# A residual quantizer with four residual buffers and a written-out order, with x stored by group and transposed two groups at a time

## The chip, the cores and the metric

The kernel runs on one core of a Trainium2 chip. The metric is the device time of one execution in microseconds; a lower time is better. TensorE is PE, VectorE is DVE, ScalarE is ACT, GpSimd is POOL and SyncE is SP in the rows of the profile.

## The reference

A depthwise convolution of three taps over time, a SiLU, four stages of residual vector quantization with eight words each, and a second depthwise convolution. The input is 2 x 16000 tokens of 512 channels in bfloat16.

```python
z = silu(conv3(x, dw_enc))                 # B=2, T=16000, D=512
res, q = z, 0
for s in range(4):                         # Nq = 4 codebooks
    cb = codebooks[s]                      # 8 words of 512
    d2 = (res*res).sum(-1) - 2*res @ cb.T + (cb*cb).sum(-1)
    sel = cb[d2.argmin(-1)]
    q, res = q + sel, res - sel
y = conv3(q, dw_dec)
```

## The kernel before, in words

The 32,000 tokens are split over 128 rows of 250 tokens. A *group* is one token of each row (128 tokens), and the 250 groups are cut into 17 *chunks* (`SIZES`, L24): 4 groups, 12 groups, fourteen times 16, and 10. A chunk's data stands with channels on the 128 partitions, in four blocks `i` of 128 channels, and the tokens along the free dimension.

Each chunk passes through these steps.

- *Load* (`load`, L419). Each group is brought by a DMA that transposes (L428), on SP's queue, into `XT`, a buffer of 34 groups by block. The first two chunks come as rows and are transposed by PE (`load_rows`, L392). `again` (L444) copies the two groups that two chunks share.
- *Front* (`front`, L464), for each block `i`: three products with the taps on VectorE (L486), written to a `Z` tile and `T` tiles. The first `SPLIT[i]` of the two additions are accumulating DMAs on POOL's queue (L497); the others are VectorE's. The second addition on VectorE (L500) writes the *residual* buffer `RES`, and so is the step that takes one of the three residual buffers. Then ScalarE makes exp (L508) into an `E` tile, VectorE adds one (L512), ScalarE takes the reciprocal (L184; exp and reciprocal need different tables, loaded by ACT_TABLE_LOAD), and VectorE multiplies (L518).
- *Stage* `s` (`stage`, L562), four times: PE computes for every 64 tokens the products with the eight words and with the tokens themselves (`score`, L584 for a mask and L590). ScalarE takes the norms (L601), VectorE casts the products (`dots`, L620), PE sums both (L604, L611), VectorE casts the sums (`VT`, L616). POOL makes the key with four operations: L658, L645, L647, L662. VectorE finds the least and the one-hot (L666, L672). PE and ScalarE turn the one-hots into pairs of words (L715, L720, L727, L733), PE selects the words (L749), and VectorE adds them to the residual: four *updates* (L755), one for each block. The fourth stage has no updates; after its scores, the residual buffer is free.
- *Finish* (`finish`, L805): PE decodes from the one-hots (L773), ScalarE copies to `YSB` (L779), and SP stores (L783).

Every operation is a task of `Plan` (L63) with an engine, a duration, the tasks that it needs, and a due time, which is the chunk's `START` plus the step's `OFF` (L38 to L60). `Plan.run` plays the tasks through while the program is built: an engine that is free takes the ready task with the earliest due time for which the buffers (`slots`) suffice. Each engine's instructions then stand in that order, and every engine works strictly in its order. Where PE has nothing to do in this play, `warm` (L382) puts in matmuls of 512 columns whose result is not used (L387), until PE is busy for the share `WARM` of 3.4 us.

The buffers are counted at L219: `plan = Plan({"Z": ZB, "T": TB, "E": EB, "Y": YB, "ps": 4, "RES": 3, "OH": 3})`, with four each of Z, T, E. A residual buffer holds for every 64 tokens 16 code columns, 64 tokens, and 16 code columns (96 columns).

Of the kernel before, what the change touches and what calls it, by code (L numbers as in the profile page):

```python
# [10 lines left out]
BF16 = mybir.dt.bfloat16  # L11
# [9 lines left out]
LC = 16  # L21
ROOM = 2 * GC + 2

SIZES = [4, 12] + [16] * 14 + [10]  # L24
# [5 lines left out]
WARM = 0.4  # L30
SPLIT = (1, 1, 1, 2)
RELU = (0, 1, 2, 3)

ZB, TB, EB, YB = 4, 4, 4, 2
# [3 lines left out]
START = [-49.78, -21.21, -11.1, 40.29, 77.41, 126.87, 171, 213.64, 259.89, 295.9, 339.35, 382.88, 414.63, 449.59, 490.48, 512.46, 542.77]  # L38
OFF = {
    "words": -209.08, "codes": -112.52, "col0": -187, "sums": -87.73, "mask": -228.88, "norms": -202.91, "col1": 18.74,  # L40
# [19 lines left out]
}  # L60


class Plan:  # L63

# [12 lines left out]
    def run(self):  # L77
# [3 lines left out]
        for n, t in enumerate(tasks):  # L81
            for d in t[3]:
                after[d].append(n)
# [789 lines left out]
```

## Time and profile before

| | us |
|---|---|
| median of 3 runs | 815.28 |
| lowest and highest run | 812.22 and 817.3 |
| the profiled execution | 809.59 |
| its span, first to last instruction | 807.8 |

The profile is that of the execution of 809.59 us; 1.8 us of it lie around the span. A row of the groups gives the line, the engine, the operation, what is written and read, the count, then the busy time and the mean of one, then the idle time of the engine just before. A row of the timeline begins with the start and the length. A window's row gives its bounds and length, the busy time and count of each engine, the granted clock of PE as a share of the full clock, the busy share of the DMA engines, and GB/s.

### The profile page before, as it was taken

Reading aid. Unit: us, or ns where it says so; the run is one execution under the profiler, and the core shown is the slowest. Engines: PE = TensorE matmul, PEld = TensorE weight load, DVE = VectorE, ACT = ScalarE, POOL = GpSimd, SP = SyncE. Lnnn points to the kernel's source line nnn. Section 1 sums busy time; section 2 is a strip of 40 time slices with the busy share of each in tenths; the row PEclk is TensorE's granted clock in tenths of the full one; section 3 lists DMA queues with packets and bytes.
Section 4 is the critical chain, followed back from the end, with each engine's and each line's share of the span. In section 5 each row is a group of like instructions: output and inputs, shape, how many; then the busy total and the mean of one; then the engine's idle time right before and its main releaser. Section 6 shows DMA issues by size and latency. Waiting matters only on the chain.

```text
span 807.8 us, 28980 instructions
## 1 busy us (share of the span) xinstructions
PE 622.8 (77%) x13019; PEld 381.0 (47%) x13092; DVE 628.2 (78%) x1027; ACT 538.6 (67%) x571; POOL 284.9 (35%) x459
## 2 busy tenths in 40 slices
PE   3065787877878878887799877878885759889985
PEld 3023454544444544535356545554553526446543
DVE  5998889896988798878778897887969785855530
ACT  2345748494789477697847976866937596793553
POOL 1244353442534155426243452253414342212200
PEclk9568788999989999989999998998998979989989
DMA  4749677767796777895967778768984542121231
GB/s 150 112 83 153 130 133 134 124 121 164 141 207 147 164 145 175 136 176 117 166 153 121 203 139 184 128 140 153 187 158 68 105 121 93 47 92 44 80 157 79
DMA packets 149542, 107.71 MB, mean 133 GB/s; under 512 B 130217, under 2 KB 131370, under 8 KB 149290
## 3 DMA queue, kind: packets, MB, share of 16 engines
q1 hardware_dynamic: 137796, 66.62, 37.4%
q0 software_dynamic: 11472, 39.10, 27.0%
q8 instruction: 102, 1.67, 0.9%
q14 instruction: 22, 0.18, 0.1%
q10 hardware_dynamic: 150, 0.13, 0.1%
HBM read 3.70 MB, written 32.77 MB: 45 GB/s over the span
## 4 chain that ended last, share of the span: by engine, by line
PE 28%; DVE 19%; ACT 14%; issue 8%; POOL 7%; DMA 3%; ACTq 0%; another core or an unknown queue 0%; DVEq 0%; POOLq 0%
PE PS L590 12%; DVE RES L755 10%; PE PS L749 5%; ACT YSB L779 4%; PE PS L584 4%; ACT E L184 3%; PE PS L773 3%; PE PS L611 2%; ACT E L508 2%; POOL S L645 2%; ACT L L601 2%; POOL D L658 2%; DVE RES L500 2%; DMA out_dram<-YSB 2%; DVE T L486 1%
## 5 line engine op out<-in xcount | busy, mean ns | idle before, releaser
L755 DVE TENSOR_TENSOR RES<-RES,PS 128x2048 bf16<-128x2048 bf16 (+2 forms) x204 | 224.5, 1136 | 26.0 <-PE PS L749 25.6
L590 PE MATMUL PS<-RES 128*64 128x80 bf16 (+1 forms) x8064 | 204.2, 208 | 36.7 <-DVE RES L518 26.7
L590 PEld LDWEIGHTS <-RES 128*64 128x64 bf16 x8064 | 170.1, 118 | 93.9 <-issue 31.7
L601 ACT ACTIVATE L<-PS 128x512 bf16<-128x512 f32 (+2 forms) x132 | 75.8, 577 | 168.5 <-PE PS L590 90.4
L749 PE MATMUL PS<-POH,PAIR 64*128 64x512 bf16 (+2 forms) x1224 | 158.4, 396 | 33.6 <-DVE RES L755 14.6
L779 ACT ACTIVATE YSB<-PS 128x1024 bf16<-128x1024 f32 (+1 forms) x126 | 124.6, 1019 | 15.3 <-PE PS L773 8.9
L184 ACT ACTIVATE E<-E 128x2048 bf16<-128x2048 bf16 (+2 forms) x68 | 120.5, 1786 | 6.6 <-DVE E L512 6.4
L658 POOL TENSOR_TENSOR D<-VT,GPOS 128x128 bf16<-128x128 bf16 (+2 forms) x68 | 45.9, 675 | 204.1 <-DVE VT L616 204.0
L749 PEld LDWEIGHTS <-PAIR 64*128 64x128 bf16 x1224 | 61.9, 102 | 103.5 <-issue 61.4
L497 POOL DMA_DIRECT2D Z<-T x75 | 73.0, 1012 | 102.7 <-issue 28.1
L508 ACT ACTIVATE E<-RES 128x2048 bf16<-128x2048 bf16 (+2 forms) x53 | 92.3, 1755 | 15.1 <-DVE RES L500 12.7
L486 DVE TENSOR_SCALAR T<-XT,WENC 128x2048 bf16<-128x2048 bf16 (+2 forms) x136 | 98.8, 739 | 3.4 <-DMA Z<-T 3.4
L773 PE MATMUL PS<-A,OHT 128*128 128x512 bf16 x224 | 80.9, 398 | 23.6 <-ACT OHT L707 5.9
L584 PE MATMUL PS<-MASK,IDENT 128*128 128x256 bf16 (+2 forms) x264 | 76.1, 288 | 12.1 <-DVE RES L755 6.0
L678 POOL COPY OH<-OH 128x128 bf16<-128x128 bf16 (+2 forms) x68 | 37.8, 562 | 121.8 <-DVE OH L672 121.7
L620 DVE CAST PR<-PS 128x64 bf16<-128x64 f32 (+2 forms) x132 | 28.8, 220 | 65.2 <-PE PS L590 50.5
L518 DVE TENSOR_TENSOR RES<-RES,E 128x2048 bf16<-128x2048 bf16 (+2 forms) x53 | 59.0, 1123 | 8.7 <-ACT E L184 8.7
L645 POOL TENSOR_SCALAR S<-VT,GMIN 128x16 f32<-128x16 bf16 (+2 forms) x68 | 51.4, 755 | 34.6 <-DVE VT L616 34.3
L500 DVE TENSOR_TENSOR RES<-Z,T 128x2048 bf16<-128x2048 bf16 (+2 forms) x53 | 63.4, 1203 | 0.1
L773 PEld LDWEIGHTS <-OHT 128*128 128x128 bf16 x373 | 32.6, 101 | 63.4 <-issue 30.2
L486 DVE TENSOR_SCALAR Z<-XT,WENC 128x2048 bf16<-128x2048 bf16 (+2 forms) x68 | 50.1, 744 | 0.2
L611 PEld LDWEIGHTS <-L 64*64 64x64 bf16 x2016 | 38.2, 111 | 20.9 <-issue 14.3
(103 smaller groups left out, 676.3 us busy)
## 6 DMA issues: line engine op xcount, KB each, us to landing
Z<-T POOLq DMA_DIRECT2D x70, 512.0 KB, 6.0
out_dram<-YSB SPq DMA_DIRECT2D x61, 512.0 KB
XT<-in_x_dram SPq DMA_TRANSPOSE x233
Z<-T POOLq DMA_DIRECT2D x5, 384.0 KB, 5.1
RES<-in_x_dram SPq DMA_DIRECT2D x1, 1536.0 KB
YSB<-in_codebooks_dram SPq DMA_DIRECT2D x12, 64.0 KB
RES<-in_x_dram SPq DMA_DIRECT2D x1, 640.0 KB
out_dram<-YSB SPq DMA_DIRECT2D x1, 384.0 KB
```

What stands on the lines that cost most here:

```text
L184: nc.scalar.add_instruction(mybir.InstActivation(name=nc.get_next_instruction_name(), engine=mybir.EngineType.Activation, ins=args, outs=[ ...
L486: nc.vector.tensor_scalar(out=u[name][:, 0:G, :], in0=XT[:, i, at + k:at + k + G, :], scalar1=WENC[:, i, k:k + 1], scalar2=None, op0=ALU.mult)
L497: nc.gpsimd.dma_start(out=z, in_=t, accum_op=ALU.add)
L500: nc.vector.tensor_tensor(out=u["R"], in0=halves(u["Z"]), in1=halves(u["ZTU"[k]]), op=ALU.add)
L508: nc.scalar.activation(halves(u["E"]), halves(u["Z"]) if adds == 2 else u["R"], ACT.Exp, scale=-1.0)
L584: nc.tensor.matmul(V[:, b, :, own:own + HT], lhsT=IDENT, rhs=MASK[:, 0:m // 2, :], start=True, stop=False, skip_group_check=True)
L590: nc.tensor.matmul(V[h * HT:(h + 1) * HT, b, r, :], lhsT=half[:, LC:LC + HT], rhs=half[:, lo:hi], start=False, stop=(i == KT - 1), skip_gr ...
L601: nc.scalar.activation(u["L", q][:, 0:m, :].rearrange("p (b r) t -> p b r t", b=2), u["V", q][:, :, :, own:own + HT], ACT.Relu)
L749: nc.tensor.matmul(u["SEL", i][:, h, 0:H * HT], lhsT=PAIR[s][rows, part, i * P:(i + 1) * P], rhs=u["POH"][rows, 0:H, :], start=(part == 0) ...
L755: nc.vector.tensor_tensor(out=tokens, in0=tokens, in1=words, op=ALU.add)
L773: nc.tensor.matmul(Y[:, h, :], lhsT=lhs(), rhs=rhs, start=(a == 0), stop=(a == len(terms) - 1))
L779: nc.scalar.activation(u["YSB"][:, k:k + n, :], u[k][:, 0:n, :], ACT.Copy)
```

## The change

The tasks stay the same in kind; what changes is where they run, in which order, and where data lies.

- Order. `START`, `OFF` and the choice by due time go. `ORDER` is a list of all task numbers, and `Plan.run` emits the tasks in it. Tiles are handed out at that time: the one of a kind that is free first.
- Buffers. There are four residual buffers (`RESN`). Their pitch falls from 96 to 80 columns for 64 tokens, since the code columns of even and odd half-groups alternate. The `E` tiles go: exp, plus one and reciprocal work in place in `Z`, of which there are seven.
- x. `XT` has the group outside, `[P, ROOM, KT, P]` for `[P, KT, ROOM, P]`, and a transfer brings two groups (`JOIN = 2`).
- Front. In chunks 2 to 15, one addition of each block is a DMA and one is VectorE's (before, block 3 had two DMAs), and the third product of blocks 2 and 3 runs on POOL (`POOLED`): 28 products. The last chunk has no product on POOL.
- Stage. The casts `dots` are ScalarE's in stages 0 and 2 (`CASTS`), and one of VectorE's or ScalarE's covers ten columns of eight. POOL's addition `S` (L645) goes: the smallest norm lies in a column of `PR` that the matmul of `total` sums. `total` starts with two matmuls of 64 rows instead of one of 128.
- PE's filling matmuls go (`WARM = 0`).
- Setup. The code columns and a part of the pair words are ScalarE's, the clearing of the decoder's tiles is POOL's, and VectorE clears PSUM once.

Line numbers of the changed kernel that are named below: products L548, the DMA add L560, the second add L562, plus one L573, silu L579, exp L570, reciprocal L224, scores L665 and L659, casts L678 and L676, `VT` L705, key L710, L714, L718, updates L817.

VectorE's order where the residual buffers turn over, before. RES_103 is the buffer, L755 the updates, L500 the add that takes the buffer for a new chunk.

```order
L755 TENSOR_TENSOR RES_103<-RES_103,PS 128x32x64 x2
L666 TENSOR_REDUCE M<-T 128x16
L755 TENSOR_TENSOR RES_103<-RES_103,PS 128x32x64
L620 CAST PR_120<-PS 128x8x8
L672 TENSOR_TENSOR OH_10494<-T,M 128x2x8x8
L486 TENSOR_SCALAR T_10496<-XT,WENC 128x2048
L620 CAST PR_120<-PS 128x8x8
L620 CAST PR_121<-PS 128x8x8
L616 CAST VT<-PS 128x144
L620 CAST PR_121<-PS 128x8x8
L500 TENSOR_TENSOR RES_103<-Z,T_10012 128x32x64
```

Between the last update of the old chunk and the first add of the new one stand four casts of scores and one product. VectorE's order at a turn of a buffer after the change; RES_138 is taken again while RES_137, RES_139 and RES_140 hold other chunks (L817 the updates, L562 the add).

```order
L817 TENSOR_TENSOR RES_138<-RES_138,PS_91 128x32x64
L548 TENSOR_SCALAR Z_103<-XT,WENC 128x2048
L722 TENSOR_REDUCE M<-KEY 128x16
L548 TENSOR_SCALAR Z_108<-XT,WENC 128x2048
L725 TENSOR_TENSOR OH_131<-KEY,M 128x2x8x8
L817 TENSOR_TENSOR RES_140<-RES_140,PS_90 128x32x64
L548 TENSOR_SCALAR Z_106<-XT,WENC 128x2048
L678 CAST PR_125<-PS_91 128x10x8
L562 TENSOR_TENSOR RES_138<-Z_104,T_110 128x32x64
```

Three products and an update of another chunk now stand there. Counted over the whole order, 163 of the 204 updates stand ahead of the last chunk's first add, and 172 before the change.

POOL's order in the middle, before: the key's operations (L658, L645, L647, L662), notes of one-hots (L678) and DMA issues (L497).

```order
L678 COPY OH_123<-OH_5579 128x16x8
L497 DMA Z<-T_5122 128x2048
L645 TENSOR_SCALAR S<-VT,GMIN 128x16
L647 TENSOR_TENSOR T<-S,STEP 128x128
L662 TENSOR_TENSOR T<-D_5584,T 128x128
L497 DMA Z<-T_5616 128x2048
L678 COPY OH_124<-OH_5769 128x16x8
L658 TENSOR_TENSOR D_5982<-VT,GPOS 128x128
```

The same after the change: the key is L710, L714, L718, the note L732, the DMA issue L560, and L548 are products.

```order
L560 DMA Z_105<-T_113 128x2048
L732 COPY OH_126<-OH_129 128x16x8
L548 TENSOR_SCALAR T_111<-XT,WENC 128x2048
L548 TENSOR_SCALAR T_110<-XT,WENC 128x2048
L710 TENSOR_TENSOR D_5075<-VT,GPOS 128x128
L714 TENSOR_TENSOR KEY<-VT,STEP 128x128
L710 TENSOR_TENSOR D_5081<-VT,GPOS 128x128
L718 TENSOR_TENSOR KEY<-D_5081,KEY 128x128
```

Two products of 2048 elements stand ahead of the next chunk's key; the S operation is gone.

The diff, cut to its core:

```diff
-SIZES = [4, 12] + [16] * 14 + [10]
+SIZES = (4, 12) + (16,) * 14 + (10,)
-WARM = 0.4
-SPLIT = (1, 1, 1, 2)
-ZB, TB, EB, YB = 4, 4, 4, 2
-START = [-49.78, -21.21, -11.1, ...
-OFF = { "words": -209.08, ...
+WARM = 0.0
+SPLIT = ((0, 0, 0, 0), (0, 0, 0, 0), (1, 1, 1, 1), (1, 1, 1, 1))
+POOLED = ((0, 0, 0, 0), (0, 0, 0, 0), (0, 0, 1, 1), (0, 0, 0, 0))
+JOIN = 2
+CASTS = (True,False,True,False)
+PSB, ZB, TB, YB, LB, POHB, RESN = 4, 7, 4, 2, 2, 2, 4
+ORDER = """
+0 40 349 351 350 38 26 30 36 34 28 32 352 8 353 355 20 357 359 9 354 179 356 358 21 ...
...
 class Plan:
+    def run(self):
+        until, end, spans = {}, {}, []
+        free = {k: [(0.0, t) for t in tiles] for k, tiles in self.free.items()}
+        order = [int(n) for n in ORDER.split()]
+        for n in order:
+            engine, hold, delay, needs, _, emit, take, give, use = self.tasks[n]
+            begin = max([until.get(engine, 0.0)] + [end[d] for d in needs])
+            for k in take:
+                at, self.held[n, k] = free[k].pop(min(range(len(free[k])), key=lambda j: free[k][j][0]))
+                begin = max(begin, at)
...
-    XT = const.tile([P, KT, ROOM, P], BF16, name="XT")
-        t = const.tile([P, KT, 2 * GC, NC + HT], BF16, name=f"RES{n}")
+    XT = const.tile([P, ROOM, KT, P], BF16, name="XT")
+        t = const.tile([P, KT, 2 * GC * WD + LC], BF16, name=f"RES{n}")
...
-            nc.sync.dma_start_transpose(out=XT[:, :, at + n, :], in_=group_rows(g0 + n - 1))
+        def some(n, m):
+            nc.sync.dma_start_transpose(out=XT[:, at + n:at + n + m, :, :].rearrange("p n k t -> p (n k) t"),
+                                        in_=bass.AP(tensor=xf.tensor, offset=xf.offset + (g0 + n - 1) * D, ap=[[S * D, P], [1, m * D]]))
...
-                nc.vector.tensor_scalar(out=u[name][:, 0:G, :], in0=XT[:, i, at + k:at + k + G, :], scalar1=WENC[:, i, k:k + 1],
+                (nc.gpsimd if k == 2 and pooled else nc.vector).tensor_scalar(out=plan.held[u[k], "Z" if k == 0 else "T"][:, 0:G, :], in0=XT[:, at + k:at + k + G, i, :],
...
-                u["E"] = epool.tile([P, GC, P], BF16, name="E")
+            def e():
+                return plan.held[u[2], "T"] if adds == 2 else z()
...
-            nc.gpsimd.tensor_scalar(out=u["S"][:, 0:G], in0=u["TR"][:, 0:G], scalar1=GMIN[:, s:s + 1], scalar2=None, op0=ALU.add)
+            if CASTS[s]:
+                nc.scalar.activation(dst, src, ACT.Copy)
+            else:
+                nc.vector.tensor_copy(dst, src)
```

More of the change, by code (lines that the diff above doesn't have):

```diff
@@ L415, in load_rows @@
-        st["loaded"] = moved + (chunks[0]["loaded"] if st["n"] else [])
-        if st["n"]:
-            codes.append(plan.add("DVE", 1.2, 1.4, moved + codes[0:1], (1, "col2"), lambda: code_columns(RESB[2])))
+            t = took[i] = plan.add("PE", 0.12 * N, 0.12 * N + 0.2, [rows], (n, "rows"), lambda i=i: turn(i), take=("ps",))
+            dve = i % 2 and n == 0
+            hold = (0.08 if dve else 0.12) * N
+            moved.append(plan.add("DVE" if dve else "ACT", hold, hold + 0.1, [t], (n, "rows"), lambda i=i: move(i), give=((t, "ps"),)))
@@ L419, in load @@
+        st["loaded"] = moved + (chunks[0]["loaded"] if n else [])
+        if n:
+            codes[2] = plan.add("ACT", 2.0, 2.2, moved + [words], (1, "col2"), lambda: code_columns(RESB[2]))
+    reads = {p: [] for p in range(ROOM)}
     def load(st):
@@ L552, in block @@
-            return rest
+                    t = plan.add("POOL", 0.9, 0.9, needs, due, lambda: total(k))
+                    return plan.add("DMA", 3.0 * f, 3.0 * f + 2.0, [t], due, None, give=give)
+                first = k == 2 and "RES" not in st
+                if k == 2:
+                    needs = needs + [st["RES"] if not first else chunks[n - 1]["RES"] if 0 < n < RESN else None]
+                t = plan.add("DVE", dve(1.13), dve(1.13) + 0.1, needs, due,
+                             lambda: total(k), take=("RES",) if first else (), give=give)
@@ new lines, in add_up @@
+                if first:
+                    st["RES"] = t
+                return t
+            hold, delay = dve(0.66), dve(0.66) + 0.1
+            for k in range(2):
+                u[k] = plan.add("DVE", hold, delay, st["loaded"], (n, f"{'ztu'[k]}{i}"), lambda k=k: product(k), take=("ZT"[k],))
+            a = add_up(1, [u[0], u[1]])
+            u[2] = plan.add("POOL" if pooled else "DVE", 0.1 + 2.2 * f if pooled else hold, 0.2 + 2.2 * f if pooled else delay, st["loaded"] + [u[1]], (n, f"u{i}"),
+                            lambda: product(2), take=("T",))
@@ L761, in stage @@
+            new.append(plan.add("DVE", 0.07 + 1.06 * f, 0.17 + 1.06 * f, [c] + seen, (n, f"U{s}{i}"), lambda i=i: update(i), give=((c, "ps"),)))
+        plan.add("FREE", 0.0, 0.0, [u["X", i] for i in range(KT)], (n, f"P{s}"), None, give=((t, "POH"),))
         st["new"] = new
-    kept = {}
     def outputs(groups, needs, n, m):
```

662 lines of the change are left out of this document (306 added, 356 removed), and 117 rows, old and new, of tables (OFF, ORDER).

## The prediction, made before the changed kernel had run

> **What bounds the kernel now.** I read the page's busy times first, then the windows, then VectorE's timeline around the residual buffers. No engine is full:
>
> ```profile
> span 807.8 us, 28980 instructions
> PE 622.8 (77%) x13019; PEld 381.0 (47%) x13092; DVE 628.2 (78%) x1027; ACT 538.6 (67%) x571; POOL 284.9 (35%) x459
> ```
>
> So something other than an engine sets the pace. The windows by stage (busy us of PE, PEld, DVE, ACT and POOL, then granted clock and DMA share; cut at the first residual add of chunk 2 and of chunk 16) and two windows of VectorE alone:
>
> ```profile
> 0.00:74.00 74.00, 30.16 (x356) 19.16 (x360) 63.57 (x158) 27.73 (x30) 22.09 (x42) 0.75 0.61 122
> 74.00:695.40 621.40, 497.58 (x10889) 306.45 (x10946) 510.94 (x777) 444.66 (x456) 245.04 (x367) 0.91 0.74 144
> 695.40:807.80 112.40, 95.09 (x1777) 55.37 (x1786) 53.74 (x95) 66.25 (x85) 17.74 (x51) 0.93 0.21 82
> ...
> 20.00:60.00 40.00, 38.77 (x85) 0.59 0.56 97
> 100.00:200.00 100.00, 84.26 (x138) 0.92 0.76 138
> ```
>
> VectorE is 97% busy from 20 to 60 us, while residual buffers are still free, and 82% (510.94 / 621.4) once all three are taken. The timeline says why. Chunk 7 takes the buffer of chunk 4, chunk 8 that of chunk 5, chunk 13 that of chunk 10; the rows show the old chunk's last update (L755), the last scores that read it (L590), and the new chunk's first add (L500):
>
> ```profile
> 326.20 3.47 DVE L755 TENSOR_TENSOR RES<-RES,PS 128x2048 bf16<-128x2048 bf16 x3
> 330.21 1.22 DVE L500 TENSOR_TENSOR RES<-Z,T 128x2048 bf16<-128x2048 bf16 x1
> ...
> 421.73 3.47 DVE L755 TENSOR_TENSOR RES<-RES,PS 128x2048 bf16<-128x2048 bf16 x3
> 426.01 0.77 PE L590 MATMUL PS<-RES 128*64 128x80 bf16 x32
> 426.95 1.22 DVE L500 TENSOR_TENSOR RES<-Z,T 128x2048 bf16<-128x2048 bf16 x1
> ...
> 544.63 2.34 DVE L755 TENSOR_TENSOR RES<-RES,PS 128x2048 bf16<-128x2048 bf16 x2
> 552.24 0.94 PE L590 MATMUL PS<-RES 128*64 128x80 bf16 x32
> 553.37 2.35 DVE L500 TENSOR_TENSOR RES<-Z,T 128x2048 bf16<-128x2048 bf16 x2
> ```
>
> Each buffer is taken again within 0.3 us of the end of its last scores (426.78 to 426.95; 553.18 to 553.37). A chunk comes every (695.4 - 74) / 14 = 44.4 us, so a buffer turns around in 3 x 44.4 = 133 us. VectorE needs only 510.94 / 14 = 36.5 of the 44.4. The buffers bound the middle; the last 112 us belong to PE (95.09 of 112.4, 85%).
>
> **The change part by part.** I cost it as VectorE's work W up to chunk 16's first add, divided by its busy share, and PE's work behind that. Today W = 63.57 + 510.94 = 574.5; 10.4 us of the first stretch are idle (74 - 63.57), and in the rest the share is 574.5 / (695.4 - 10.4) = 84%.
>
> ```profile
> L486 DVE TENSOR_SCALAR T<-XT,WENC 128x2048 bf16<-128x2048 bf16 x112 | 85.7, 777 | 3.4 <-DMA Z<-T 3.4
> L500 DVE TENSOR_TENSOR RES<-Z,T 128x2048 bf16<-128x2048 bf16 x42 | 54.5, 1304 | 0.1
> L620 DVE CAST PR<-PS 128x64 bf16<-128x64 f32 x112 | 24.8, 223 | 53.4 <-PE PS L590 42.8 <-ACT L L601 10.1
> L249 DVE COPY RES<-CBT 128x2048 bf16<-128x2048 bf16 x3 | 2.3, 778 | 0.0
> L250 DVE COPY RES<-CBT 128x2048 bf16<-128x2048 bf16 x3 | 3.1, 1039 | 0.0
> L331 DVE COPY YSB<-PAIR 128x512 uint16<-128x512 uint16 x3 | 1.4, 458 | 0.1
> L342 DVE COPY YSB<-YSB 128x512 uint16<-128x512 uint16 x3 | 1.3, 439 | 0.0
> ```
>
> VectorE loses 28 products to POOL (28 x 0.777 = -21.8), gains 14 second adds that the POOL queue's accumulating DMA did (14 x 1.304 = +18.3), gives 56 of 112 casts to ACT (-12.5), and the setup copies of the last four rows (-8). The new memsets of PSUM fall into its idle start: 0.
>
> POOL's products are not shown before. The nearest rows are a copy of half the size, same type, and a two-input one of 512 f32; and VectorE beside POOL's long operations:
>
> ```profile
> L444 POOL COPY XT<-XT x7: 1027/1037/2072, 54.4 to 551.5; 128x1024 bf16<-128x1024 bf16 x7
> L344 POOL TENSOR_TENSOR PAIR<-YSB 128x512 bf16<-128x512 f32 x3 | 5.0, 1664 | 0.0
> ...
> 42.75 1.57 POOL L344 TENSOR_TENSOR PAIR<-YSB 128x512 bf16<-128x512 f32 x1
> 43.13 1.62 DVE L486 TENSOR_SCALAR Z<-XT,WENC 128x1536 bf16<-128x1536 bf16 x1
> 44.67 0.61 DVE L486 TENSOR_SCALAR T<-XT,WENC 128x1536 bf16<-128x1536 bf16 x1
> ...
> 205.36 2.07 POOL L444 COPY XT<-XT 128x1024 bf16<-128x1024 bf16 x1
> 205.32 1.21 DVE L500 TENSOR_TENSOR RES<-Z,T 128x2048 bf16<-128x2048 bf16 x1
> 206.84 1.67 DVE L500 TENSOR_TENSOR RES<-Z,T 128x2048 bf16<-128x2048 bf16 x1
> ```
>
> Length: 2 x 1.037 = 2.1 us, bounded above by 4 x 1.664 = 6.7; I take 2.1, one input and the same type. Beside POOL's 1.57 us, VectorE's product grew by 1.01 us (64% of it); beside its 2.07 us, an add grew by 0.46 (22%). I take the mean, 43%: 28 x 2.1 x 0.43 = +25, between 0 (POOL runs while VectorE reads PSUM) and the whole, +59. What the offload saves is lost to this. The Trainium skill, page "SBUF — State Buffer", section "Who interferes with whom", calls the port pair that VectorE and GpSimd share an exclusive lock; the 1.62 us row agrees. Taken as the whole length of every product it gives a rival of its own, below.
>
> The fourth buffer moves the front ahead: in the new order VectorE stands at 163 updates of 204 when chunk 16 makes its first add, and at 172 in the old. Nine updates leave W, each 1.2 us with 0.3 of its stage's casts: -13. W = 574.5 - 21.8 + 18.3 - 12.5 - 8 + 25 - 13 = 562.5.
>
> The share is the main choice. Its ends are 84% (as now) and 97% (20 to 60 us, buffers free). With four buffers, a turn of 133 us would allow a chunk every 33 us, less than the 36.5 that VectorE needs, so the buffers stop binding and engines wait for each other instead: PE would be at 475 / 625 = 76%, ACT near 72%. I take 90%, halfway: 562.5 / 0.90 = 625, and with the idle start 635.4 against 695.4.
>
> ```profile
> 74.00:695.40 621.40, 22.61 (x60) 6.50 (x71) 0.91 0.74 144
> 695.40:807.80 112.40, 5.06 (x17) 1.69 (x19) 0.93 0.21 82
> 695.40:807.80 112.40, 34.56 (x32) 0.93 0.21 82
> ```
>
> These are the filling matmuls (L387: 22.61 and 5.06 us of PE) and the updates left at the end (L755: 32). The fillers go; where they stood PE is idle anyway, so I count nothing. The tail has 41 updates for 32. PE's useful 90.0 us there are 2.81 an update: 41 x 2.81 = 115, at the same 85%: 136 us against 112.4. The front's lead is partly given back here.
>
> Covered edits:
>
> ```profile
> L428 SPq DMA_TRANSPOSE XT<-in_x_dram x233: 1190/1269/3372, 23.0 to 604.2; - x117
> 33.69 0.69 DVE L250 COPY RES<-CBT 128x2048 bf16<-128x2048 bf16 x1
> L184 ACT ACT_TABLE_LOAD x24 | 30.8, 1283 | 0.4
> L720 ACT ACTIVATE OHT<-PS 128x128 bf16<-128x128 f32 x42 | 11.5, 274 | 9.5 <-PE PS L715 9.4
> L645 POOL TENSOR_SCALAR S<-VT,GMIN 128x16 f32<-128x16 bf16 x56 | 44.7, 799 | 26.7 <-DVE VT L616 26.4
> ```
>
> - Half as many transposes move the same bytes; SP is the only queue that they pass, and VectorE's products wait for none of them now (their only idle time, 3.4 us, is for Z<-T). If each double one took as long as two, nothing changes; the cover is that x lies a chunk ahead.
> - Products read 16 runs of 128 instead of one of 2048. L250 writes runs of 16 at 0.69 us for 2048, no slower than the products: 0. The upper end, the 1.304 of an add, would be +0.53 a product.
> - ACT gets 66 casts (274 ns: +18) and some 12 us of setup copies; table loads fall from 47 to 33 (14 x 1.283: -18). It has room.
> - POOL loses S (-51 with the small forms) and 15 DMA issues, and gets 59 us of products. Stage steps queued behind two products in a row come up to 4 us late; with four chunks in flight another chunk is ready.
>
> Sum: 635.4 + 136 + 1.8 around the span = 773, against 809.6 for the profiled execution. The median of the runs, 815.28, is 0.7% above that execution, so I predict 778.
>
> **The rivals.** (a) *Slower: POOL's products stop VectorE for long.* For: the 1.62 us row, and that an instruction with a scalar from memory is not in the trace. The gain is gone when W reaches 595, that is at 2.1 us of stopped VectorE for each product. At 4 us and 64% it is 2.6: W = 609, 677 + 10.4 + 136 + 1.8 = 825, 831 for the runs. Against: the nearest row of the same type gives 2.1 us a product, of which 43% are 0.9. (b) *Every product stops VectorE for exactly its 2.1 us*, which is the skill's rule at its strictest: W = 596.5, 811, 817 for the runs: no change. Against: the 22% row. (c) *The buffers weren't it*: the share stays at 84%, since waits for PE's scores only move: 670 + 10.4 + 136 + 1.8 = 818, 824 for the runs. Against: buffers re-taken within 0.3 us, and the 97%. (d) *PE's clock falls without the fillers*: the 0.59 at 20 to 60 us shows what idleness does. At 0.80, PE's 475 us become 540; with a share of 87% and a tail of 158 this is 817, 822 for the runs. Against: the fillers are 3.6% of the middle. (e) *The share reaches 97%*: 580 + 10.4 + 136 + 1.8 = 728, 733 for the runs.
>
> **How the numbers follow.** My forecast (750 to 805) 0.42; (e) 0.15; (a) 0.14; (b) 0.09; (c) 0.13; (d) 0.07. About 1% is what a measurement can tell, so no change is 807 to 823. Faster by over 1%: the forecast, (e), and the better half of (c) and (d): 0.65. Within 1%: 0.16. Slower: (a) and the worse part of (c): 0.19. The range runs from (e) to (a): 733 to 831.
>
> **What would show it.** Right: from 60 to 600 us VectorE near 90%; chunk 16's first add near 635 us; some 136 us behind it with PE above 80%; POOL's products near 2.1 us, and VectorE's products and adds beside them up to twice as long. Wrong: first adds that still wait for scores with VectorE near 84% (c); products over 4 us (a); granted clock in the middle at 0.8 (d); idle VectorE before products that ends with XT's transfer.

## The result and the profile after

The changed kernel takes 845.02 us (median; 841.07 to 856.99) against 816.51 us of the kernel before: 1.0345 times, with a 95% interval of 1.0304 to 1.0387. I had predicted 778 us and a range up to 831. The change makes the kernel slower by 28 us, and the time is 67 us above the forecast.

The rows of the changed kernel are from a second profile of it (run after_again below, an execution of 844.07 us), since the first was of its longest execution, 856.99 us. Its span and engines:

```profile
span 842.3 us, 28865 instructions
PE 612.0 (73%) x12963; PEld 384.4 (46%) x13031; DVE 696.2 (83%) x919; ACT 545.1 (65%) x640; POOL 399.0 (47%) x411
```

VectorE was to lose work; it has 696.2 us of it where it had 628.2. The windows, cut as in the prediction at the first residual add (now L562) of chunk 2 and of chunk 16 (busy us of PE, PEld, DVE, ACT, POOL, then granted clock, DMA share, GB/s):

```profile
0.00:60.80 60.80, 10.38 (x126) 9.00 (x127) 44.30 (x106) 33.08 (x37) 16.70 (x41) 0.78 0.73 141
60.80:713.90 653.10, 488.87 (x10363) 307.10 (x10417) 584.08 (x702) 435.46 (x491) 360.71 (x314) 0.82 0.60 124
713.90:842.30 128.40, 112.78 (x2486) 68.25 (x2494) 67.86 (x114) 76.53 (x113) 21.63 (x57) 0.97 0.21 83
```

VectorE's work W up to chunk 16's first add is 44.3 + 584.1 = 628.4 us (predicted 562.5), its share after the idle start is 628.4 / (713.9 - 10.4) = 89% (predicted 90%), and the tail is 128.4 us (predicted 136). So the share and the tail came as forecast, and W did not. VectorE's large groups, and GpSimd's products:

```profile
L817 DVE TENSOR_TENSOR RES<-RES,PS 128x2048 bf16<-128x2048 bf16 x168 | 199.8, 1213 | 21.9 <-PE PS L811 19.2 <-ACT L L669 1.1 <-ACT Z L570 0.6
L548 POOL TENSOR_SCALAR T<-XT,WENC 128x2048 bf16<-128x2048 bf16 x28 | 166.5, 5970 | 8.9 <-DVE RES L562 8.9
...
L579 DVE TENSOR_TENSOR RES<-RES,Z 128x2048 bf16<-128x2048 bf16 x56 | 86.4, 1547 | 1.7 <-ACT Z L224 1.7
L548 DVE TENSOR_SCALAR T<-XT,WENC 128x2048 bf16<-128x2048 bf16 x84 | 80.5, 960 | 1.0 <-DMA Z<-T 1.0
L562 DVE TENSOR_TENSOR RES<-Z,T 128x2048 bf16<-128x2048 bf16 x56 | 79.0, 1422 | 2.0 <-POOL T L548 1.8 <-DMA Z<-T 0.2
L573 DVE TENSOR_SCALAR Z<-Z 128x2048 bf16<-128x2048 bf16 x56 | 58.6, 1057 | 0.1
L548 DVE TENSOR_SCALAR Z<-XT,WENC 128x2048 bf16<-128x2048 bf16 x56 | 56.1, 1009 | 0.1
```

A product on GpSimd takes 5.97 us, not 2.1. The updates (L817), which read PSUM, keep their 1.21 us; the other groups of VectorE here, which work on SBUF alone, have longer means than in the run after_dve below. GpSimd and VectorE in one place show how:

```profile
473.93 12.36 POOL L548 TENSOR_SCALAR T<-XT,WENC 128x2048 bf16<-128x2048 bf16 x2
...
474.17 4.78 DVE L817 TENSOR_TENSOR RES<-RES,PS 128x2048 bf16<-128x2048 bf16 x4
480.99 4.65 DVE L579 TENSOR_TENSOR RES<-RES,Z 128x2048 bf16<-128x2048 bf16 x1
```

Two products stand one behind the other. Four updates out of PSUM run through beside the first in 4.78 us, as ever; the multiplication of two SBUF tensors beside the second takes 4.65 us, nearly four times as long as usual, and ends at 485.64, 0.65 us before GpSimd's second product (486.29).

### The profile page after: what moved, and what is told of

Same layout as the page of the kernel before. It is cut to its first block, busy times and chain, and to the rows that moved or that the text cites. A ratio compares the mean times of both kernels' runs of the same rounds, so it can differ in the third digit from the quotient of the medians.

```text
span 855.2 us, 28933 instructions
## 1 busy us (share of the span) xinstructions
PE 626.3 (73%) x13031; PEld 387.1 (45%) x13031; DVE 696.3 (81%) x919; ACT 544.8 (64%) x640; POOL 398.6 (47%) x411
## 5 line engine op out<-in xcount | busy, mean ns | idle before, releaser
L817 DVE TENSOR_TENSOR RES<-RES,PS 128x2048 bf16<-128x2048 bf16 (+2 forms) x204 | 226.9, 1136 | 36.2 <-PE PS L811 33.1
L665 PE MATMUL PS<-RES 128*64 128x72 bf16 (+1 forms) x8064 | 219.9, 213 | 32.5 <-DVE RES L579 18.7
L665 PEld LDWEIGHTS <-RES 128*64 128x64 bf16 x8064 | 184.5, 122 | 104.5 <-issue 45.7
L548 POOL TENSOR_SCALAR T<-XT,WENC 128x2048 bf16<-128x2048 bf16 x28 | 166.5, 5969 | 8.7 <-DVE RES L562 8.7
L845 ACT ACTIVATE Y<-PS 128x1024 bf16<-128x1024 f32 x126 | 124.6, 1018 | 61.5 <-PE PS L841 51.9
L669 ACT ACTIVATE L<-PS 128x512 bf16<-128x512 f32 (+2 forms) x132 | 75.2, 577 | 101.0 <-PE PS L665 60.9
L570 ACT ACTIVATE Z<-RES 128x2048 bf16<-128x2048 bf16 (+2 forms) x68 | 119.3, 1782 | 25.2 <-DVE RES L562 25.1
L224 ACT ACTIVATE Z<-Z 128x2048 bf16<-128x2048 bf16 (+2 forms) x68 | 120.5, 1784 | 9.5 <-DVE Z L573 9.3
L560 POOL DMA_DIRECT2D Z<-T x60 | 55.0, 949 | 140.1 <-issue 44.6
L841 PE MATMUL PS<-A,FIN 128*128 128x512 bf16 x249 | 91.6, 413 | 16.2 <-DVE RES L817 7.2
L579 DVE TENSOR_TENSOR RES<-RES,Z 128x2048 bf16<-128x2048 bf16 (+2 forms) x68 | 96.7, 1427 | 5.9 <-ACT Z L224 5.9
L548 DVE TENSOR_SCALAR T<-XT,WENC 128x2048 bf16<-128x2048 bf16 (+2 forms) x108 | 97.8, 910 | 2.5 <-DMA Z<-T 2.4
L659 PE MATMUL PS<-MASK,IDENT 128*128 128x256 bf16 (+2 forms) x264 | 78.5, 298 | 24.9 <-DVE RES L817 21.4
L710 POOL TENSOR_TENSOR D<-VT,GPOS 128x128 bf16<-128x128 bf16 (+2 forms) x68 | 47.1, 694 | 105.1 <-DVE VT L705 105.0
L562 DVE TENSOR_TENSOR RES<-Z,T 128x2048 bf16<-128x2048 bf16 (+2 forms) x68 | 89.0, 1323 | 2.8 <-POOL T L548 1.9
L714 POOL TENSOR_TENSOR KEY<-VT,STEP 128x128 f32<-128x128 bf16 (+2 forms) x68 | 50.4, 742 | 85.7 <-DVE VT L705 85.7
L732 POOL COPY OH<-OH 128x128 bf16<-128x128 bf16 (+2 forms) x68 | 34.5, 509 | 75.2 <-DVE OH L725 75.2
L573 DVE TENSOR_SCALAR Z<-Z 128x2048 bf16<-128x2048 bf16 (+2 forms) x68 | 64.6, 959 | 0.1
L548 DVE TENSOR_SCALAR Z<-XT,WENC 128x2048 bf16<-128x2048 bf16 (+2 forms) x68 | 63.6, 942 | 0.0
L841 PEld LDWEIGHTS <-FIN 128*128 128x128 bf16 x373 | 32.1, 104 | 65.7 <-issue 44.0
```

The source lines that it names most:

```text
L224: nc.scalar.add_instruction(mybir.InstActivation(name=nc.get_next_instruction_name(), engine=mybir.EngineType.Activation, ins=args, outs=[ ...
L548: (nc.gpsimd if k == 2 and pooled else nc.vector).tensor_scalar(out=plan.held[u[k], "Z" if k == 0 else "T"][:, 0:G, :], in0=XT[:, at + k:a ...
L562: nc.vector.tensor_tensor(out=residual(), in0=halves(z()), in1=halves(t), op=ALU.add)
L570: nc.scalar.activation(halves(e()), halves(z()) if adds == 2 else residual(), ACT.Exp, scale=-1.0)
L579: nc.vector.tensor_tensor(out=residual(), in0=halves(z()) if adds == 2 else residual(), in1=halves(e()), op=ALU.mult)
L659: nc.tensor.matmul(banked(q, m // 2)[:, b, :, LC:], lhsT=IDENT, rhs=MASK[:, 0:m // 2, :], start=True, stop=False, skip_group_check=True)
```

## The experiments

The theory of the lock: GpSimd's products hold what VectorE needs for operands in SBUF. Its rivals: the written order with its buffers and layout costs the time by itself, or GpSimd's queue is what delays. Ratios are to the kernel before on the same chip, with their 95% intervals in brackets.

**The changed kernel again (after_again).**

> The changed kernel itself, unchanged, for a second profile of it. Every theory: 841 to 847 us. The theory of the lock (GpSimd's 28 third products of 5.97 us, working beside VectorE, keep VectorE from its own SBUF operands) wants 28 products of 5.4 to 7.3 us again, and VectorE about 690 us busy with 90 to 100 us of it stretched instructions. The theory of the order (the written order, the fourth residual buffer and the layout cost the time, the products little) would have VectorE's instructions about as long when no product runs as when one does.

845.02 us, 1.0338 (1.0277 to 1.0399). Products of 5.97 us, VectorE 696.2 us busy: the rows above.

**Products back on VectorE (after_dve).** Everything else of the change stays.

```
-POOLED = ((0, 0, 0, 0), (0, 0, 0, 0), (0, 0, 1, 1), (0, 0, 0, 0))
+POOLED = ((0, 0, 0, 0),) * 4
```

> The changed kernel with the 28 third products back on VectorE at the same places of the same written order. Theory of the lock: VectorE's work up to chunk 16's first add goes from 628 by -95 (stretch) and +28 x 0.777 = +22 to 555 us; at the share of 88 to 90 per cent and with chunk 2's first add at 62 the end is at 765 to 785 us, below the kernel before. Theory of the order: VectorE has 22 us more to do and the rest stays, so 830 to 870 us. A third, that GpSimd's queue is what delays (keys, notes and DMA issues behind two products in a row): also near 775, but then VectorE's busy time does not fall by 70 and its idle time does.

776.87 us, 0.9523 (0.9436 to 0.961). The page, the windows with the same cuts, and the same groups:

```profile
span 773.2 us, 28816 instructions
PE 601.5 (78%) x12963; PEld 378.0 (49%) x13031; DVE 624.4 (81%) x947; ACT 544.0 (70%) x640; POOL 237.8 (31%) x383
```

```profile
0.00:61.20 61.20, 11.42 (x126) 10.09 (x127) 45.15 (x106) 33.11 (x37) 16.68 (x41) 0.78 0.71 140
61.20:641.10 579.90, 474.69 (x10365) 298.89 (x10419) 511.52 (x730) 434.42 (x491) 199.52 (x286) 0.86 0.71 139
641.10:773.20 132.10, 115.40 (x2484) 68.98 (x2493) 67.75 (x114) 76.48 (x113) 21.57 (x57) 0.94 0.21 81
```

```profile
L548 DVE TENSOR_SCALAR T<-XT,WENC 128x2048 bf16<-128x2048 bf16 x112 | 84.4, 761 | 0.1
L562 DVE TENSOR_TENSOR RES<-Z,T 128x2048 bf16<-128x2048 bf16 x56 | 69.7, 1255 | 2.0 <-DMA Z<-T 1.9
L579 DVE TENSOR_TENSOR RES<-RES,Z 128x2048 bf16<-128x2048 bf16 x56 | 68.7, 1230 | 2.9 <-ACT Z L224 2.9
L548 DVE TENSOR_SCALAR Z<-XT,WENC 128x2048 bf16<-128x2048 bf16 x56 | 42.4, 764 | 0.1
L573 DVE TENSOR_SCALAR Z<-Z 128x2048 bf16<-128x2048 bf16 x56 | 41.9, 758 | 0.0
```

With 28 more products, VectorE has 72 us less to do. What GpSimd's products take from it is 696.2 + 28 x 0.777 - 624.4 = 93.6 us, 3.34 for each, 56% of their 166.5. W falls by 71.7 (628.4 to 556.7) and chunk 16's first add by 72.8 (713.9 to 641.1): one for one. The theory of the order falls: the same order is faster than the kernel before. So does the queue as the cause here: the time sits in VectorE's instructions.

**Half of them on GpSimd (after_one).**

```
-POOLED = (..., (0, 0, 1, 1), ...)
+POOLED = (..., (0, 0, 0, 1), ...)
```

> The changed kernel with block 3's third product alone on GpSimd (14 of the 28). If each product costs by itself, by what it takes from VectorE: half of the 68 us between no product and 28, 805 to 817 us. If it is the second of two in a row that costs (keys and notes behind 12 us of GpSimd's queue): 777 to 795 us.

799.56 us, 0.9845 (0.9755 to 0.9936): 22.7 above no product, a third of the 68, between the two expectations. VectorE's loss is 656.7 + 14 x 0.777 - 624.4 = 43.2 us, 3.1 for each, so each product does cost by itself; its first add of chunk 16 comes only 25.2 us later (666.3) for 32.2 us more of W, so a part fell into idle time. The other 14 cost more than their work: from here to the changed kernel W grows by 39.5 us and the first add comes 47.6 us later (666.3 to 713.9). That the two agree over all 28 is the sum of these halves.

**The products by themselves (products_alone).** The stretch ahead of the setup, in its order on GpSimd:

```python
nc.gpsimd.tensor_scalar(out=T[0], in0=Z[0], scalar1=SC, scalar2=None, op0=ALU.mult)
nc.gpsimd.tensor_scalar(out=T[1], in0=Z[0], scalar1=0.5, scalar2=None, op0=ALU.mult)
nc.gpsimd.tensor_copy(T[2], Z[0])
nc.gpsimd.tensor_tensor(out=T[3], in0=Z[0], in1=Z[0], op=ALU.mult)
...
nc.vector.tensor_scalar(out=Z[2], in0=Z[1], scalar1=SC, scalar2=None, op0=ALU.mult)   # ten times
```

> The changed kernel with a stretch put ahead of its setup (its results go nowhere): four operations of GpSimd on 128x2048 bf16 with VectorE still (product with the tap from SBUF, with a constant, a plain copy, a product of two tensors), then one product on GpSimd at a time beside ten of VectorE's products, eight of its adds of two tensors, sixteen of its copies out of PSUM. Prediction's length: 2.1 us alone, and then 5.97 us is 2.1 us of work plus waiting for VectorE. Other theory: the product itself is 4 to 6 us long on GpSimd, with nothing beside it. Lock: beside a product one or more of VectorE's instructions on SBUF alone last 4 us and more while its copies out of PSUM keep their length; no lock: each of VectorE's is stretched by some tenths alike.

This version ran once (908.58 us), and only its rows are used (start, us, engine, line), GpSimd's first, then VectorE's:

```profile
6.51 5.45 POOL L270 TENSOR_SCALAR T<-Z,SC 128x2048 bf16<-128x2048 bf16 x1 [4.78 <-DVE Z L269]
11.96 6.67 POOL L271 TENSOR_SCALAR T<-Z 128x2048 bf16<-128x2048 bf16 x1
18.58 2.33 POOL L272 COPY T<-Z 128x2048 bf16<-128x2048 bf16 x1
20.89 3.59 POOL L273 TENSOR_TENSOR T<-Z 128x2048 bf16<-128x2048 bf16 x1
...
26.10 5.86 POOL L275 TENSOR_SCALAR T<-Z,SC 128x2048 bf16<-128x2048 bf16 x1
...
6.79 1.76 DVE L269 MEMSET Z<- 128x2048 bf16 x1 [0.37 <-issue]
...
13.59 5.57 DVE L277 TENSOR_SCALAR Z<-Z,SC 128x2048 bf16<-128x2048 bf16 x1
...
27.07 5.44 DVE L277 TENSOR_SCALAR Z<-Z,SC 128x2048 bf16<-128x2048 bf16 x1
```

Beside memsets alone, which take 1.76 us with it and without it, a product with a scalar takes 5.45 us. A plain copy of the same size takes 2.33 us, near the 2.1 of the prediction's rows, and a product of two tensors 3.59. So 5.45 of the 5.97 us are the operation's own. Beside VectorE's products and adds it takes 5.45 to 7.05 us with the tap (three of them) and 6.27 and 6.67 with a constant, so this run does not tell tap and constant apart. What goes beyond 5.45 I read as GpSimd waiting for VectorE in its turn: in the changed kernel a product that began while a multiplication of VectorE ran took 6.28 us (at 516.37; the multiplication ended at 517.33), and one that began beside updates out of PSUM 5.44 (at 562.60). The Trainium skill, page "GPSIMD Engine Reference", section "3.1 Elementwise — side-by-side cycle accounting", gives 1.03 cycles an element for the shortest bodies; at its 1.2 GHz that is 1.8 us for 2048 by my estimate. The 5.45 us of this row disagrees, and the measurement decides.

The four products of VectorE that come beside one of GpSimd last 5.44 to 6.58 us, and three of them end some 0.55 us after GpSimd's (27.07 + 5.44 = 32.51 against 26.10 + 5.86 = 31.96). An add of two SBUF tensors lasts 4.55 us and ends 0.65 us before GpSimd's product (54.42 + 4.55 against 53.35 + 6.27), as the multiplication above does. The copies out of PSUM moved behind the products in the order, so that part was not seen here; the four updates above show it.

**A shorter form on GpSimd (after_tt).**

```
-nc.gpsimd.tensor_scalar(out=T, in0=XT, scalar1=WENC[:, i, k:k + 1], scalar2=None, op0=ALU.mult)
+nc.gpsimd.tensor_tensor(out=T, in0=XT, in1=<WENC[:, i, k:k + 1] repeated>, op=ALU.mult)
```

> The changed kernel with GpSimd's 28 products written as a product of two tensors, the second the tap repeated along the row. Alone, such an instruction took 3.59 us, the product with a scalar 5.45. If what VectorE loses goes with GpSimd's time: 3.6 to 4.5 us each, of which 0.56 is lost, 57 to 71 us in place of 94, W 591 to 605 in place of 628, and 803 to 820 us in place of 845. If each product costs the same whatever its length (a stop and a start, or the order around it): 845 us.

825.39 us, 1.0142 (1.0025 to 1.026), just above the 803 to 820 of the theory. Its product and its page:

```profile
L549 POOL TENSOR_TENSOR T<-XT,WENC 128x2048 bf16<-128x2048 bf16 x28 | 106.9, 3848 | 9.9 <-DVE RES L566 9.9
```

```profile
PE 604.7 (74%) x12963; PEld 377.7 (46%) x13031; DVE 677.5 (83%) x919; ACT 544.6 (67%) x640; POOL 346.2 (42%) x411
```

The length counts: 3.85 us instead of 5.97, and VectorE loses 677.5 + 21.8 - 624.4 = 74.9 us. That is 70% of GpSimd's time, not 56%, hence the miss. One place of the order shows a reason, after_again first, then after_tt:

```profile
562.60 5.44 POOL L548 TENSOR_SCALAR T<-XT,WENC 128x2048 bf16<-128x2048 bf16 x1
563.61 3.77 DVE L579 TENSOR_TENSOR RES<-RES,Z 128x2048 bf16<-128x2048 bf16 x1
...
539.78 3.60 POOL L549 TENSOR_TENSOR T<-XT,WENC 128x2048 bf16<-128x2048 bf16 x1
540.82 3.65 DVE L583 TENSOR_TENSOR RES<-RES,Z 128x2048 bf16<-128x2048 bf16 x1
```

Beside the product with a scalar, VectorE's multiplication ends 0.66 us before GpSimd's instruction; beside the product of two tensors it ends 1.09 us after it. GpSimd's shorter form holds it almost as long as the longer one. How much of the 70% this makes up was not added up.

**Products on ScalarE (after_act).**

```
-nc.gpsimd.tensor_scalar(out=T, in0=XT, scalar1=WENC[:, i, k:k + 1], scalar2=None, op0=ALU.mult)
+nc.scalar.activation(T, XT, ACT.Copy, scale=WENC[:, i, k:k + 1])
```

> The changed kernel with the same 28 third products on ScalarE (a copy with the tap as its scale), at the same places of the order. Theory of the lock: ScalarE's copies do not stretch VectorE, VectorE's work up to chunk 16's first add is 628 - 95 = 533 us; at a share of 85 to 88 per cent (ScalarE's 28 x 1.9 us lie ahead of exponentials and evictions) 745 to 780 us. Theory of the order: 820 to 860 us. If ScalarE's products stretched VectorE as GpSimd's do, VectorE's other products would again have means of 0.95 us rather than 0.74.

801.23 us, 0.9781 (0.9707 to 0.9856): slower than expected. ScalarE stretches nothing (VectorE's other products have a mean of 0.76 us and its busy time is 604.4 us, 20 less than with the products on it), and still the end is 24 us later. ScalarE's products take 2.00 us each, in its order, ahead of what the stages wait for: VectorE waits 11.2 us for the products themselves, and 30.6 us instead of 21.8 for the norms (L669 in the waits of after_dve further down). That VectorE's work divided by a fixed share gives the time holds only while the links between the engines stay.

**One part alone in the kernel before (before_pool).** The instruction is placed as before; only its engine differs.

```
-nc.vector.tensor_scalar(out=u[name][:, 0:G, :], ...
+(nc.gpsimd if k == 2 and i > 1 and 1 < n < 16 else nc.vector).tensor_scalar(out=u[name][:, 0:G, :], ...
```

> The kernel before with one thing of the change: the third products of blocks 2 and 3 in chunks 2 to 15 (28) on GpSimd. Theory of the lock: VectorE's busy time goes from 628 by -22 and +28 x 5.97 x 0.56 = +94 to 700 us; up to chunk 16's first add 574.5 + 72 = 646, which is 836 us at a share of 0.92 and 893 at the 0.84 of before: 835 to 895 us. Theory of the order (products on GpSimd cost little where the order is not the new one): 795 to 820 us.

917.39 us, 1.1263 (1.1184 to 1.1342): worse than either theory. Its page and two of VectorE's waits:

```profile
PE 650.9 (71%) x13019; PEld 391.9 (43%) x13092; DVE 647.4 (71%) x999; ACT 540.1 (59%) x571; POOL 429.9 (47%) x487
```

```profile
DVE M L666 <- POOL T L662: 46.3, 33, 6.5
DVE RES L500 <- POOL T L486: 44.7, 7, 12.7
```

VectorE loses 647.4 + 21.8 - 628.2 = 41 us to the lock here, less than half of what it loses in the changed kernel and 26% of the 155.6 us that GpSimd's products take, so its work grows by 19 us net. Most of the 101 us is waiting: for the products themselves (44.7 us, none before) and for keys behind them (46.3 us, 26.6 before), and for what comes late after these. In this order, which was made for products on VectorE, waiting costs more than the lock.

**Terms of the sum: the clock (dve_fill, rows_fill).**

```
-WARM = 0.0
+WARM = 0.4
```

> All products on VectorE, and the fillers of TensorE back (the constant for them 0.4 as before). Theory of the clock: the granted clock of the middle goes from 0.86 towards 0.91, TensorE's 475 us there become 450, and what VectorE waits for TensorE (some 60 us) shrinks by about a tenth to a third: 757 to 772 us in place of 777. Rival: the fillers stand in the way of work that is due, 777 to 790 us. Neither: within 4 us of 777.

778.04 us, 0.9557 (0.9421 to 0.9693). The granted clock goes from 0.866 to 0.897, and the time shows no gain beyond its scatter (769 to 790 us, and 773 to 784 in after_dve); a gain of about 1% would be hidden in it. Once more on the fastest version (below):

> The fastest so far (products on VectorE, all dots on ScalarE, codebook rows from ScalarE's queue, 755.8 us) with the fillers of TensorE. Theory of the clock: now that VectorE has less to do, TensorE's clock (0.88 in the middle) counts: 740 to 752 us. As with the products on VectorE alone, nothing: 752 to 759 us.

757.45 us, 0.9266 (0.9182 to 0.935), against 755.76: no gain either, with a scatter of 753 to 771 us.

**The copies of the dots (dve_nocast, before_cast, dve_allcast, dve_allsums).** In the three runs of the changed kernel the products are on VectorE.

```
-CASTS = (True,False,True,False)
+CASTS = (False,) * 4        dve_nocast
+CASTS = (True,) * 4         dve_allcast; dve_allsums has SUMS = (True,) * 4 as well
```

> All products on VectorE, and the dots of stages 0 and 2 copied by VectorE again (as before) rather than by ScalarE. The prediction's sum (VectorE's work over its share): 66 copies of 0.24 us are 16, of them 13 ahead of chunk 16's first add, over 0.88: 777 + 15 = 792 us. Rival: the copies on ScalarE stand behind exponentials of 1.9 us and cost the chain of stages as much as they save, so within 5 us of 777 or below.

824.61 us, 1.0115 (1.0033 to 1.0197): 48 us for 66 copies that are 11 us more of VectorE's busy time (635.6 against 624.4). VectorE's waits of after_dve, then of dve_nocast (us, times, longest):

```profile
DVE RES L817 <- PE PS L811: 29.6, 33, 4.5
DVE PR L678 <- ACT L L669: 21.8, 18, 2.7
DVE VT L705 <- PE PS L696: 19.0, 14, 3.4
...
DVE PR L678 <- PE PS L665: 12.7, 9, 5.4
```

```profile
DVE PR L678 <- ACT L L669: 37.1, 30, 3.9
DVE VT L705 <- PE PS L696: 33.3, 25, 3.4
DVE RES L817 <- PE PS L811: 30.0, 39, 2.7
DVE PR L678 <- PE PS L665: 28.8, 19, 4.8
```

The waits for scores and sums grow by 46 us. A copy in VectorE's queue stops all that stands behind it until TensorE and ScalarE are there; in this order its 0.24 us are the small part. Neither the sum nor its rival had this size.

In the kernel before, the same edit (in `stage`), with one more buffer for the norms:

```
-nc.vector.tensor_copy(u["PR"][:, q:q + m, 0:C]..., u["V", q][:, :, :, pick:pick + C])
+if s in (0, 2): nc.scalar.activation(dst, src, ACT.Copy)
+else: nc.vector.tensor_copy(dst, src)
...
-b = plan.add("DVE", 0.06 + 0.01 * m, ...)
+b = plan.add("ACT" if s in (0, 2) else "DVE", 0.06 + 0.01 * m, ...)
...
-dpool = ctx.enter_context(tc.tile_pool(name="dpool", bufs=3))
+dpool = ctx.enter_context(tc.tile_pool(name="dpool", bufs=4))
```

> The kernel before with one thing of the change: the dots of stages 0 and 2 copied by ScalarE (and four buffers instead of three for what ScalarE leaves of a score). In the kernel before VectorE is idle for 64.6 us ahead of its 132 copies, since a copy stands in its queue until TensorE's scores are there. Theory of the stop (what a copy on VectorE costs is the wait in its queue, not its 0.22 us): half of the 64.6 us and of the work goes, 770 to 795 us. The prediction's sum: only the work, 66 x 0.22 = 15 us over 0.9, 800 us. Rival: the next instruction of the chain (the copy of the sums, or an update) waits instead: 808 to 817 us.

In the kernel before, where the order is planned anew with these copies on ScalarE, it gives nothing: 817.22 us, 0.9951 (0.9907 to 0.9995). The theory of the stop does not hold there: the updates and the least then wait (VectorE's waits ahead of L759 and L670, as they are numbered there, are 42.3 and 35.0 us, 25.6 and 26.6 before).

> All products on VectorE, and the dots of all four stages copied by ScalarE. Theory of the stop: VectorE's 66 copies that are left have 36.5 us of waiting ahead of them and 15.7 us of work; with them gone 730 to 752 us. The prediction's sum: 15.7 us over 0.88, 759 us. Rival: the copy of the sums waits in their place, and ScalarE's queue is longer: 770 to 785 us.

766.7 us, 0.9413 (0.9312 to 0.9515): 10 us below after_dve, with intervals that overlap, and less than the sum's 18. The copy of the sums waits 41.3 us instead of 19.0, and one product waits 9.32 us for an accumulating DMA (at 210.07), where the longest such wait of after_dve has 1.9.

> As the one above, and the copies of the sums of all four stages on ScalarE as well (68 of 0.30 us, with 19 us of waiting ahead of them on VectorE). Theory of the stop: 15 to 35 us below the run above. Sum: 68 x 0.3 = 20 us over 0.88, 23 us below it. Rival: a copy on ScalarE comes up to 1.9 us later (behind an exponential or a reciprocal) 68 times in a chain that GpSimd waits for: as the run above, or slower by up to 40 us.

795.0 us, 0.9744 (0.9664 to 0.9825): 28 us slower for 20 us less work on VectorE; the rival. Updates wait 82.0 us for TensorE and the least 50.6 us for the key, which hangs on a copy in ScalarE's queue.

**One group to a transfer (dve_single, single_stores, single_pool).** Products on VectorE; two transfers at the place of one.

```
-nc.sync.dma_start_transpose(out=XT[:, at + n:at + n + m, :, :]..., in_=...)
+for j in range(m):
+    nc.sync.dma_start_transpose(out=XT[:, at + n + j, :, :], in_=...)
```

> All products on VectorE, and one group to a transposing transfer (two transfers at the place of one). VectorE never waited for a transposed group in the changed kernel: within 4 us of 777. If SyncE's queue or the transfers' fixed part counted, the first groups of chunks 2 and 3 would come later and VectorE would wait for them: 785 to 800 us.

815.9 us, 0.9991 (0.9947 to 1.0035): 39 us, where I expected none. VectorE waits for no transposed group in this run either. SyncE's transposes in after_dve, then those of dve_single with one place of its queue and a wait of ScalarE:

```profile
L487 SPq DMA_TRANSPOSE XT<-in_x_dram x117: 1232/1309/5626, 2.5 to 565.6; - x117
```

```profile
L488 SPq DMA_TRANSPOSE XT<-in_x_dram x233: 1188/1267/3617, 2.5 to 608.5; - x117
```

```profile
299.16 25.58 SPq L488 DMA_TRANSPOSE XT<-in_x_dram  x16
324.87 1.19 SPq L850 DMA_DIRECT2D out_dram<-Y  x1
```

```profile
ACT Y L846 <- DMA out_dram<-Y: 35.2, 9, 10.4
```

A transfer of two groups holds SyncE as long as one of one (medians of 1.31 and 1.27 us). With single groups a store stands behind 16 of them, and ScalarE waits 35.2 us (4.0 in after_dve) for the store's buffer. I read the rest as a chain: ScalarE's queue holds up TensorE, and TensorE VectorE, whose updates wait 55.3 us for TensorE (29.6 in after_dve). I took the stores off SyncE twice (`nc.sync.dma_start(out=outv...` becomes `nc.scalar` and `nc.gpsimd`):

> All products on VectorE, one group to a transposing transfer (816 us), and the stores of the output issued from ScalarE's queue instead of SyncE's. Theory of the queue: with single groups 16 transposes hold SyncE for 25.6 us in a row, the stores stand behind them, ScalarE waits 35 us for a store's buffer, TensorE and VectorE wait for ScalarE; freed from that, 777 to 795 us (62 issues of some 0.4 us are new on ScalarE). Theory of the transfers (twice as many transposes load the transfer engines): 808 to 820 us.

826.24 us, 1.0142 (1.0077 to 1.0207): ScalarE's own stores now wait for transposes that have not landed; ScalarE stands idle for 53.3 us until these land.

> All products on VectorE, one group to a transposing transfer, and the stores of the output issued from GpSimd's queue. From ScalarE's queue they waited 53.3 us for transposes that had not landed, so that run did not tell the queue from the transfers. Theory of the queue: freed from standing behind 16 transposes on SyncE, 780 to 800 us (62 issues of some 0.95 us are new on GpSimd, whose keys stand behind them). Theory of the transfers: 808 to 825 us, and ScalarE still waits some 35 us for a store's buffer.

807.68 us, 0.9884 (0.9821 to 0.9948): ScalarE's wait for a store's buffer is down to 6.7 us, but GpSimd's keys stand behind stores that wait for ScalarE, and VectorE waits 41.9 us for them (15.7 in after_dve). Whichever queue takes the stores pays. That the 39 us come from SyncE's queue is what the rows of dve_single suggest; these two runs do not settle it, and twice as many transfers as the cause is not ruled out.

**The idle start (allcast_rows).** dve_allcast, with the loads of the codebook rows on ScalarE's queue.

```
-nc.sync.dma_start(out=W[h * HT:(h + 1) * HT, at, :],
+nc.scalar.dma_start(out=W[h * HT:(h + 1) * HT, at, :],
```

> All products on VectorE, all dots copied by ScalarE (767 us), and the twelve loads of the codebook rows issued from ScalarE's queue, where they do not stand behind the first transposes, which hold SyncE from 2.5 to 13.6 us. VectorE waits 11.9 us for the first of these rows. If that wait is on the path: 755 to 761 us, chunk 2's first add at 50 to 55 us in place of 60.6. If the next wait takes its place (the first rows of x): 764 to 769 us.

755.76 us, 0.9286 (0.9214 to 0.9359), the fastest version. VectorE's first use of these rows in dve_allcast, then in this run:

```profile
20.26 0.29 DVE L380 TENSOR_SCALAR PAIR<-Y 128x512 uint16<-128x512 uint16 x1 [11.92 <-DMA Y<-in_codebooks_dram]
```

```profile
15.60 0.29 DVE L380 TENSOR_SCALAR PAIR<-Y 128x512 uint16<-128x512 uint16 x1 [7.39 <-DMA Y<-in_codebooks_dram]
```

The wait shrinks by 4.5 us only (chunk 2's first add at 56.0, not 50 to 55), and the end comes 11 us earlier, with intervals that overlap: the first add of chunk 16 is at 619.9 instead of 630.9. For the other 6 us the traces offer the 9.32 us wait of dve_allcast for a DMA, which this run does not have; no run separates the two.

## Why the prediction was wrong

- **The step that failed** is the price of GpSimd's products: "28 x 2.1 x 0.43 = +25". The length was read from a plain copy as "one input and the same type"; a copy of 2048 does take 2.33 us, but a product with a scalar takes 5.45 beside memsets alone and 5.97 in the kernel. The part that VectorE loses was 43% by two rows and is 56%. So the term is 93.6 us, and W is 628.4 instead of 562.5. With W put right, the prediction's own formula gives 628.4 / 0.90 + 10.4 + 136 + 1.8 = 846 us.
- **The two rows behind the 43%** were misread as shares. The 1.62 us product starts 0.38 us after GpSimd's operation and ends 0.43 us after it (44.75 against 44.32): it was held for all that was left, and 64% says only how late it came. In the other pair GpSimd's copy lasts 2.07 us where the median of its line is 1.04: it had itself been held by the first add (205.32 to 206.53), and only the rest of it could hold the second. So the 22% was no evidence for a mild stop.
- **Rival (a) is what happened**, with the sign at the place it named: the gain is gone at 2.1 us of stopped VectorE for each product, and 3.34 were measured. Its own price, 4 us at 64%, was too low, and so was the range. I had written down an upper bound of 6.7 us; at 64% that is 120 us, and the range should have reached there. An operation of which the trace shows no row deserved more than 0.14.
- **Rival (b)**, whole length and no more, was wrong in length, not in kind: a product of VectorE on SBUF is held until GpSimd's product ends, one of two SBUF tensors until shortly before, and updates that read PSUM are not held. The 4.78 us of four updates show why the loss can stay below the whole length. The Trainium skill, page "SBUF — State Buffer", section "Who interferes with whom", says that the loser blocks for the whole instruction; the 5.44 us row agrees, and the 4.65 us row, which ends 0.65 us before GpSimd's, does so only in part.
- **The other terms of W were right together**: without GpSimd's products the formula's W is 562.5 - 25 + 21.8 = 559.3, and after_dve has 556.7.
- **The share**: 90% predicted, 88% in after_dve (556.7 / (641.1 - 10.4)), 89% in the changed kernel. It is right as a number, but its reason, that the fourth buffer frees the middle, is not shown. The prediction's row of L500 has 0.1 us of idle time ahead of the 42 adds that take a buffer; if the buffers bound the old kernel, the wait stood ahead of the casts before these adds (53.4 us in its row of L620), and that stays open. Taking the dots' copies or the paired transfers away brings the same four buffers back to 824.6 and 815.9. The fourth buffer alone was not tried: the written order needs it.
- **The tail**: 136 us predicted with 115 of TensorE; 132.1 with 115.4 in after_dve, 128.4 with 112.8 after.
- **The casts**, "-12.5" as work, were worth 48 us in this order and nothing in the old one. **The paired transfers**, "if each double one took as long as two, nothing changes", are worth 39 in this order: I looked for who waits for x and not for who stands behind it in SyncE's queue, the stores, which the rows of dve_single point to.
- **Rival (d)**: its sign came, a granted clock of 0.82 in the middle where it had been 0.91, but not its price: TensorE's work there is 488.9 us, not 540. With the products back on VectorE and no fillers the clock is 0.866 over the whole run, with the fillers 0.897, so the fillers explain a part of the fall from 0.897 to 0.84. Bringing them back shows no gain in time. **The layout**: products by group take 0.76 us, no more than before.
- **The idle start** of 10.4 us is 16.5, with a wait for codebook rows behind the first transposes; on the path if the 11 us of allcast_rows hold, but small.

That the sum for products on VectorE, 559.3 / 0.90 + 10.4 + 136 + 1.8 = 770 us, comes within 7 us of 776.87 owes something to parts that only work together.

## What to carry to other kernels

An operation that moves to another engine needs a row of that very operation there; the estimate from a plain copy was 2.1 us, and the product took 5.97. GpSimd's time next to VectorE is not free time: of what GpSimd's products took, VectorE lost 56% and 70% in the changed order, and 26% in the old one, where VectorE was busy for 71% of the span instead of 83%. In a written-out order a short instruction costs what stands behind it, so ask of each queue what waits in it, stores and copies too.

## What the runs showed of the hardware

- On GpSimd, 128x2048 bf16: copy 2.33 us, product of two tensors 3.59, product with a scalar from memory 5.45 beside memsets alone; 5.45 to 7.05 us with tap or constant beside VectorE's work. The product with a scalar is the slowest of the three.
- Beside GpSimd's product with a scalar, a VectorE product on SBUF ends some 0.55 us after it (5.44 us for one of 0.7), an add or multiplication of two SBUF tensors 0.65 us before it (4.55 and 4.65 us for one of 1.2); beside GpSimd's product of two tensors such a multiplication ends 1.09 us after it. Updates that read PSUM (1.21 us each) and memsets (1.76 us) do not notice.
- A transposing transfer of two groups holds SyncE for 1.31 us (median), one of one group for 1.27.
